# The first row tile of a LayerNorm, FNet and SwiGLU kernel loaded in two halves, with ten warm-up matmuls for eleven

## The chip, the cores and the metric

The kernel runs on one core of a Trainium2 chip. The metric is the device time of one execution in microseconds, given as the median of several runs. The engines in the text are TensorE (PE in the profile, its weight loads PEld), VectorE (DVE), ScalarE (ACT), GpSimd (POOL) and SyncE (SP), which issues most of the loads.

## The reference

`x` has S = 2048 rows of D = 640, F is 1536. `re` and `im` are DFT matrices.

```python
xn = _layernorm(x, axis=-1)                       # (x - m) / sqrt(v + 1e-5) over each row
a = einsum("bsd,ed->bse", xn, dft_hid_re)
b = einsum("bsd,ed->bse", xn, dft_hid_im)
s = einsum("ts,bse->bte", dft_seq_re, a) - einsum("ts,bse->bte", dft_seq_im, b)
h = (_silu(xn @ w_gate) * (xn @ w_up)) @ w_down
return x + s * _silu(h)
```

## The kernel before, in words

The kernel first multiplies the sequence matrices by `xn` (four passes, `seq(0)` to `seq(3)`), then applies the hidden matrices (`hid_s`), then gate, up and down, and adds `x`. Large products are split by Strassen's scheme. Almost every product is made of three matmuls: each operand is split into a high and a low part (tiles `hl`), high by ScalarE (`hl<-raw` or `hl<-xn`, ACTIVATE) and low by VectorE (TENSOR_TENSOR or SCALAR_TENSOR_TENSOR).

A planner (`Plan`) sets the order. Each operation is added with the keys that it reads and writes; `prod` adds one that must be done by a lead time, `step` one of TensorE. In `seq(0)` the plan is `fixed`: operations stand at written times. `pl.alias` lets one key stand for several.

The change lies in `opening()`, which is the start of `seq(0)`. Row tile k of `x` is 128 rows by 640 columns of float32, 320 KB. `OPEN_DMA` lists the first loads in order, all issued by SP: (0,) is row tile 0, (0, 0) the first two blocks of the real sequence matrix `in_cs`, (1, 0) those of the imaginary one, and so on:

```python
OPEN_DMA = ((0,), (0, 0), (1,), (1, 0), (2,), (3,), (0, 1), (1, 1), (4,), (5,), (0, 2), (1, 2), ...)
```

SP's loads use eight semaphores in turn (`DMAHW0` to `DMAHW7`), and a load waits until the one eight places before it, with the same semaphore, has landed.

`layer_norm` works on one row tile: two `bn_stats` of 320 columns each and one `bn_aggr` on VectorE, a square root on ScalarE, one small operation on GpSimd, and small VectorE operations for the scale and the mean. For row tile 0 VectorE then writes `neg`, the negated normalised columns 0 to 255, and normalises the last 128 columns in place. These are the weights of the first six float32 products (kk = 0), which aren't split: three with the block of the real matrix and three with that of the imaginary one. A float32 product is two records in the trace, called passes here. From row tile 1 on (kk = 1 to 7) the operands are split.

Ahead of the first product, `busy(ps[:, 7], n)` issues n warm-up matmuls, 128x512 in bfloat16, of a tile `z` of zeros. Their result isn't used.

All operations are recorded at line 82, so the tiles tell them apart in the profile.

Of the kernel before, what the change touches and what calls it, by code (L numbers as in the profile page):

```python
# [14 lines left out]
P = 128  # L15
# [263 lines left out]
def tile_fnet_swiglu(  # L279
# [16 lines left out]
    nc = Probe(tc.nc)  # L296
# [5 lines left out]
    pl = Plan()  # L302
    mv = one.tile([P, NS, 2], F32, name="mv")
    sm = one.tile([P, 6, NS], F32, name="sm")
    bst = one.tile([P, 2, 2, 6], F32, name="bst")
# [5 lines left out]
    ps = psum.tile([P, 8, TC], F32, name="ps")  # L311
# [3 lines left out]
    def raw(name, a=0, n=None):  # L315
        o, (arena, size) = where[name], pl.size[name]
        n = size - a if n is None else n
        over = arena == "raw" and o >= RAW_KB * 256 - 8
        return space["raw3" if over else arena][:, o + a - over * (RAW_KB * 256 - 8):][:, :n]
# [235 lines left out]
    xn = pl.buf(("xn",), "raw2", NS * D)  # L555
# [5 lines left out]
    def xn_tile(k):  # L561
        return space["xn", k // 8][:, k % 8 * D:k % 8 * D + D]

    def load_x(k, lead, eng):
        pl.prod(lead, lambda: eng.dma_start(xn_tile(k), x[k * P:(k + 1) * P, :]), [], [(xn, k)])

    def layer_norm(k0, n, lead, root, stats, small):

        for k in range(k0, k0 + n):
            for h in range(2):
                pl.prod(stats[k - k0], lambda k=k, h=h: nc.vector.bn_stats(
                    bst[:, k % 2, h], xn_tile(k)[:, h * 320:h * 320 + 320]), [(xn, k)], [("bst", k % 2, h)])
            pl.prod(stats[k - k0], lambda k=k: nc.vector.bn_aggr(
                mv[:, k], bst[:, k % 2].rearrange("p a b -> p (a b)")),
                [("bst", k % 2, 0), ("bst", k % 2, 1)], [("mv", k)])
        y, t, mr, v, nm = (sm[:, i, k0:k0 + n] for i in range(5))
        mean, var = (mv[:, k0:k0 + n, i] for i in range(2))  # L580
        r = rowst[:, 0, NS + k0:NS + k0 + n]
        key = ("sm", k0)
        if small is nc.vector and n == 1:
            sign, half = (-1.0, nm) if k0 == 0 else (1.0, r)
            ops = [
                lambda: nc.scalar.activation(t, var, AF.Sqrt, bias=sm[:, 5, 4:5], scale=0.25),
                lambda: nc.gpsimd.tensor_scalar(v, var, EPS, 0.25 * sign, op0=ALU.add, op1=ALU.mult),
                lambda: small.reciprocal(y, t),
                lambda: small.scalar_tensor_tensor(v, v, y, t, op0=ALU.mult, op1=ALU.subtract if k0 == 0 else ALU.add),
                lambda: small.reciprocal(half, v),  # L590
            ]
            if k0:
                ops.append(lambda: small.scalar_tensor_tensor(mr, mean, -1.0, r, op0=ALU.mult, op1=ALU.mult))
        elif small is nc.vector:
            stt = small.scalar_tensor_tensor
            ops = [
                lambda: nc.scalar.activation(t, var, AF.Sqrt, bias=sm[:, 5, :1]),
                lambda: small.reciprocal(y, t),
                lambda: stt(t, var, EPS, y, op0=ALU.add, op1=ALU.mult),
                lambda: stt(t, t, -0.5, y, op0=ALU.mult, op1=ALU.mult),  # L600
                lambda: stt(r, t, 1.5, y, op0=ALU.add, op1=ALU.mult),
                lambda: stt(mr, mean, -1.0, r, op0=ALU.mult, op1=ALU.mult),
            ]
        else:
            ops = [
                lambda: small.tensor_scalar(v, var, EPS, 1.0, op0=ALU.add, op1=ALU.mult),
                lambda: small.tensor_tensor(y, v, sm[:, 5, 8:8 + n], op=ALU.pow),
                lambda: small.tensor_scalar(nm, mean, -1.0, 0.0, op0=ALU.mult, op1=ALU.add),
                lambda: small.tensor_tensor(t, v, y, op=ALU.mult),
                lambda: small.tensor_tensor(t, t, y, op=ALU.mult),  # L610
                lambda: small.tensor_scalar(t, t, -0.5, 1.5, op0=ALU.mult, op1=ALU.add),
                lambda: small.tensor_tensor(r, y, t, op=ALU.mult),
                lambda: small.tensor_tensor(mr, nm, r, op=ALU.mult),
            ]
        for i, fn in enumerate(ops):
            pl.prod(root[i > 0], fn, [("mv", k) for k in range(k0, k0 + n)], [key])
        if k0 == 0:
            neg = pl.buf(("neg",), "raw", 256)
            minus = lambda to, a, n, scale: small.tensor_scalar(to, xn_tile(0)[:, a:a + n], mean, scale, op0=ALU.subtract, op1=ALU.mult)
            for e in range(2):  # L620
                pl.prod(root[2], lambda e=e: minus(raw(neg, e * P, P), e * P, P, nm), [(xn, 0), key], [(neg, 0)])
            pl.prod(root[2], lambda: small.tensor_scalar(r, nm, -1.0, 0.0, op0=ALU.mult, op1=ALU.add), [key], [key])
            pl.prod(root[2], lambda: minus(xn_tile(0)[:, TC:], TC, P, r), [(xn, 0), key], [(xn, 0, 2)])
            pl.prod(root[2], lambda: small.tensor_tensor(mr, mean, nm, op=ALU.mult), [key], [key])
            pl.prod(lead[0], lambda: nc.scalar.activation(
                xn_tile(0)[:, :TC], xn_tile(0)[:, :TC], AF.Identity, bias=mr, scale=r), [key, (xn, 0), (neg, 0)], [(xn, 0, 0), (xn, 0, 1)])
            return neg
        for k in range(k0, k0 + n):
            pl.prod(lead[k - k0], lambda k=k: nc.scalar.activation(
                xn_tile(k), xn_tile(k), AF.Identity, bias=sm[:, 2, k:k + 1], scale=rowst[:, 0, NS + k:NS + k + 1]),  # L630
                [key, (xn, k)], [(xn, k, c) for c in range(3)])

    def busy(bank, n):

        for _ in range(n):
            nc.tensor.matmul(bank, z[:, :P], z, start=True, stop=True)
# [105 lines left out]
    def seq(k):  # L742
# [112 lines left out]
        def opening():  # L855
# [3 lines left out]
            at = lambda t: -t  # L859
# [7 lines left out]
            def fetch(i, g, t, a=None):  # L867
                src = cs[j, i, g // 2, :, 2 * (g % 2):2 * (g % 2) + 2]
                name = left[i, g]
                if a is None:  # L870
                    pl.prod(at(t), lambda: nc.sync.dma_start(wide(raw(name)), src), [], [(name, 0), (name, 1)])
                else:
                    pl.prod(at(t), lambda: nc.sync.dma_start(raw(name, a * TC, TC), src[:, a]), [], [(name, a)])

            t = -6.0
            for what in OPEN_DMA:
                if len(what) == 1:
                    load_x(what[0], at(t), nc.sync)
                else:
                    fetch(what[0], what[1], t, *what[2:])  # L880
                t += 0.45
            neg = [layer_norm(k0, n, [at(x) for x in apply], [at(x) for x in root], [at(x) for x in stats], nc.vector)
                   for k0, n, stats, root, apply in OPEN_LN][0]
            for kk in range(1, 8):
# [9 lines left out]
            for kk in range(8):  # L894
                for i, banks, db in part if kk < 7 else part[::-1]:
# [6 lines left out]
                    o, a = (s[i, 1], 0) if kk == 1 else (s[i, kk // 2 * 2], kk % 2)  # L902
# [23 lines left out]
        def p2(g):  # L926
            if fresh:
                for kk in (8 + 2 * g, 9 + 2 * g):
                    load_x(kk, 40 + 2 * g, nc.sync)
                layer_norm(8 + 2 * g, 2, *LEAD["xn", 4 + g], nc.gpsimd)  # L930
            return operand("p2", g, load(12, g, 11 if fresh else 20, "raw"))
# [19 lines left out]
        if fresh:  # L951
            opening()
        elif not shared:
            run(("p1", p1, b2, (1, 1)))
# [413 lines left out]
    for i, (t, _, fn, names, _) in enumerate(pl.ops):  # L1368
        if i == turn:
            last.close()  # L1370
            first.close()
            space["hl2"], space["hl3"] = (stack.enter_context(tc.tile_pool(name=name, bufs=1, reuse_waits="tile")).tile(
                [P, TURN_KB * 256], F32R, name=name) for stack, name in ((ctx, "hl2"), (last, "hl3")))
        if i == back:
            last.close()
            space["raw3"] = ctx.enter_context(tc.tile_pool(name="raw3", bufs=1, reuse_waits="tile")).tile(
                [P, TURN_KB * 256], F32, name="raw3")
        if t >= 0 and not started:
            started = True
            busy(ps[:, 7], 11)  # L1380
        fn()


# [38 lines left out]
```

## Time and profile before

| | us |
|---|---|
| median of 3 runs (lowest to highest) | 969.77 (969.72 to 969.93) |
| the profiled execution | 969.83 |
| its span | 967.6 |

| engine | busy us | share of the span |
|---|---|---|
| PE | 961.7 | 99% |
| PEld | 792.0 | 82% |
| DVE | 734.6 | 76% |
| ACT | 488.6 | 50% |
| POOL | 121.3 | 13% |

Times in the profile are microseconds from the start of the span. In the timeline a row is: start, duration, engine (SPq is SyncE's queue), line, operation, output and input tiles, shapes and count, and in brackets the idle time of the engine ahead of it with what ended it. Neighbouring rows of a kind are merged, and how far depends on the stretch that is asked for. In the chain of waits a row is start, duration and what. In a table by stretches of time the row has the length, then the busy time of PE, PEld, DVE, ACT and POOL, the granted clock, the busy share of the DMA engines and what they moved in GB/s.

### The profile page before, as it was taken

The numbers are of one execution on the slowest core, as the hardware profiler recorded it, in microseconds if no ns is written. First come the engines' busy times: TensorE is split into PE (matmuls) and PEld (weight loads), VectorE is DVE, ScalarE is ACT, GpSimd is POOL, SyncE is SP. The second block draws the span as 40 slices with busy tenths as digits, with TensorE's granted clock in tenths as the row PEclk, the third lists the DMA queues.
The fourth block names the chain that finished last, engine by engine and source line by source line (L and its number), as shares of the span: only waits on it lengthen the run. The fifth ranks groups of instructions, "written<-read, shape, count | busy, mean of one in ns | idle before, by whom it ended". The sixth has DMA issues, their size and how long they took to land.

```text
span 967.6 us, 11521 instructions
## 1 busy us (share of the span) xinstructions
PE 961.7 (99%) x4235; PEld 792.0 (82%) x4235; DVE 734.6 (76%) x932; ACT 488.6 (50%) x676; POOL 121.3 (13%) x184
## 2 busy tenths in 40 slices
PE   9999999999999999999999999999999999999998
PEld 5888888888888888888888888888888888888887
DVE  7889668757774687676987898999978666666775
ACT  5686445454545455544356555563446444444341
POOL 1460211011101110111100211210002000000000
PEclk9999999999999999999999999999999999999999
DMA  9997848494938497778673374439699330105793
GB/s 352 283 249 215 233 147 229 152 271 106 231 109 255 109 236 263 208 196 253 170 213 131 141 265 155 168 136 289 222 292 256 99 133 4 55 1 163 240 346 131
DMA packets 64056, 186.50 MB, mean 193 GB/s; under 512 B 6528, under 2 KB 10368, under 8 KB 64000
## 3 DMA queue, kind: packets, MB, share of 16 engines
q1 hardware_dynamic: 45952, 125.45, 39.0%
q0 software_dynamic: 18048, 60.32, 24.2%
q8 instruction: 33, 0.54, 0.2%
q14 instruction: 23, 0.19, 0.1%
HBM read 151.39 MB, written 34.36 MB: 192 GB/s over the span
## 4 chain that ended last, share of the span: by engine, by line
PE 99%; DMA 0%; DVE 0%; ACT 0%; issue 0%; DVEq 0%; ACTq 0%
PE ps L82 99%; DMA xn<-in_x 0%; DVE raw L82 0%; DVE bst L82 0%; DVE sm L82 0%; ACT raw L82 0%; ACT sm L82 0%; DVE mv L82 0%; DVEq L82 0%; ACTq L82 0%
## 5 line engine op out<-in xcount | busy, mean ns | idle before, releaser
L82 PE MATMUL ps<-hl 128*128 128x512 f32 (+1 forms) x3258 | 780.1, 388 | 0.0
L82 PEld LDWEIGHTS ps<-hl 128*128 128x128 f32 x3258 | 610.1, 188 | 126.6 <-DVE hl L82 0.6
L82 DVE TENSOR_TENSOR hl<-raw,hl 128x1024 fp32r<-128x1024 f32 (+5 forms) x360 | 346.5, 994 | 134.3 <-ACT hl L82 94.4
L82 ACT ACTIVATE hl<-raw 128x1024 fp32r<-128x1024 f32 (+6 forms) x416 | 325.0, 826 | 170.3 <-DVE raw L82 84.8
L82 PE MATMUL ps<-hl,hl 128*128 128x512 f32 (+1 forms) x954 | 259.9, 388 | 0.0
L82 ACT ACTIVATE raw<-ps 128x512 f32<-128x512 f32 (+1 forms) x144 | 97.9, 681 | 231.4 <-PE ps L82 225.2
L82 PEld LDWEIGHTS ps<-hl,hl 128*128 128x128 f32 x954 | 179.0, 188 | 36.9
L82 DVE TENSOR_TENSOR raw<-raw 128x1024 f32<-128x1024 f32 (+7 forms) x216 | 178.6, 849 | 19.8 <-ACT raw L82 15.5
L82 DVE TENSOR_TENSOR raw<-ps,raw 128x512 f32<-128x512 f32 (+1 forms) x95 | 77.2, 814 | 48.4 <-PE ps L82 47.6
L82 DVE TENSOR_TENSOR raw<-raw,raw 128x512 f32<-128x512 f32 (+3 forms) x50 | 44.2, 892 | 6.5 <-ACT raw L82 4.3
L82 ACT ACTIVATE hl<-xn 128x1024 fp32r<-128x1024 f32 (+3 forms) x61 | 42.2, 723 | 13.6 <-PE ps L82 9.1
L82 POOL DMA_DIRECT2D p_dram<-raw x24 | 16.4, 686 | 251.4 <-DVE raw L82 215.7
L82 ACT ACTIVATE raw<-raw 128x512 f32<-128x512 f32 (+1 forms) x30 | 21.5, 718 | 46.7 <-DVE raw L82 46.7
L82 DVE TENSOR_TENSOR hl<-xn,hl 128x1024 fp32r<-128x1024 f32 (+3 forms) x50 | 40.8, 833 | 4.0 <-PE ps L82 3.9
L82 POOL DMA_DIRECT2D raw<-in_cs x36 | 32.5, 984 | 57.7 <-DMA raw<-in_cs 29.1
L82 DVE SCALAR_TENSOR_TENSOR hl<-raw,hl 128x256 fp32r<-128x256 f32 (+4 forms) x56 | 32.7, 586 | 4.0 <-ACT hl L82 4.0
L82 POOL DMA_DIRECT2D out<-raw x10 | 6.9, 689 | 226.6 <-DVE raw L82 197.3
L82 POOL DMA_DIRECT2D d_p<-hl x28 | 15.2, 543 | 71.4 <-ACT hl L82 59.6
L82 ACT ACTIVATE xn<-xn,sm,rowst 128x640 f32<-128x640 f32 (+1 forms) x16 | 14.1, 906 | 5.3 <-DVE sm L82 3.6
L82 DVE BATCH_NORM_STATS2 bst<-xn 128x6 f32<-128x320 f32 x32 | 13.7, 479 | 4.0 <-DMA xn<-in_x 4.0
L82 POOL DMA_DIRECT2D y_dram<-raw x12 | 8.2, 683 | 64.6 <-DVE raw L82 46.2
L82 POOL DMA_DIRECT2D raw<-p_dram x8 | 10.1, 1267 | 44.7 <-DVE raw L82 26.3
(42 smaller groups left out, 84.3 us busy)
## 6 DMA issues: line engine op xcount, KB each, us to landing
raw<-in_cs SPq DMA_DIRECT2D x84, 512.0 KB, 7.0
hl<-d_p SPq DMA_DIRECT2D x56, 384.0 KB, 5.0
raw<-in_cs POOLq DMA_DIRECT2D x36, 512.0 KB, 9.8
raw<-in_wb SPq DMA_DIRECT2D x24, 640.0 KB, 4.7
d_p<-hl POOLq DMA_DIRECT2D x28, 384.0 KB, 4.0
p_dram<-raw POOLq DMA_DIRECT2D x16, 512.0 KB, 4.4
raw<-p_dram SPq DMA_DIRECT2D x8, 768.0 KB, 8.5
xn<-in_x SPq DMA_DIRECT2D x16, 320.0 KB, 9.8
```

The costliest lines, as they stand in the source:

```text
L82: return real(*args, **kw)
```

## The change

Row tile 0 is loaded as two halves of 320 columns. Each has a key of its own, (xn, 0, "a") and (xn, 0, "b"); the alias makes an operation that reads the whole tile wait for both, and each of the tile's two `bn_stats` reads one. The other loads follow in the same order. The warm-ups go from eleven to ten.

```diff
+    pl.alias[xn, 0] = [(xn, 0, "a"), (xn, 0, "b")]
+
-    def load_x(k, lead, eng):
-        pl.prod(lead, lambda: eng.dma_start(xn_tile(k), x[k * P:(k + 1) * P, :]), [], [(xn, k)])
+    def load_x(k, lead, eng, h=None):
+        if h is None:
+            pl.prod(lead, lambda: eng.dma_start(xn_tile(k), x[k * P:(k + 1) * P, :]), [], [(xn, k)])
+        else:
+            pl.prod(lead, lambda: eng.dma_start(xn_tile(k)[:, h * 320:h * 320 + 320], x[k * P:(k + 1) * P, h * 320:h * 320 + 320]),
+                    [], [(xn, k, "ab"[h])])
...
                 pl.prod(stats[k - k0], lambda k=k, h=h: nc.vector.bn_stats(
-                    bst[:, k % 2, h], xn_tile(k)[:, h * 320:h * 320 + 320]), [(xn, k)], [("bst", k % 2, h)])
+                    bst[:, k % 2, h], xn_tile(k)[:, h * 320:h * 320 + 320]), [(xn, k) if k else (xn, k, "ab"[h])], [("bst", k % 2, h)])
...
             for what in OPEN_DMA:
-                if len(what) == 1:
+                if len(what) == 1 and what[0] == 0:
+                    for h in range(2):
+                        load_x(0, at(t + 0.2 * h), nc.sync, h)
+                elif len(what) == 1:
                     load_x(what[0], at(t), nc.sync)
...
-            busy(ps[:, 7], 11)
+            busy(ps[:, 7], 10)
```

On SP, at the start of the program, this stood in a row before (`xn_108` is the tile that holds row tiles 0 to 7, 128x1024 a pair of blocks of `in_cs`; what a load waits for stands in brackets):

```order
L82 DMA xn_108<-in_x 128x640
L82 DMA raw<-in_cs 128x1024
L82 DMA xn_108<-in_x 128x640
L82 DMA raw<-in_cs 128x1024
L82 DMA xn_108<-in_x 128x640 x2
L82 DMA raw<-in_cs 128x1024 x2
L82 DMA xn_108<-in_x 128x640 [waits DMAHW0_49]
L82 DMA xn_108<-in_x 128x640 [waits DMAHW1_49]
L82 DMA raw<-in_cs 128x1024 [waits DMAHW2_49]
L82 DMA raw<-in_cs 128x1024 [waits DMAHW3_49]
```

And this stands there now:

```order
L82 DMA xn_108<-in_x 128x320 x2
L82 DMA raw<-in_cs 128x1024
L82 DMA xn_108<-in_x 128x640
L82 DMA raw<-in_cs 128x1024
L82 DMA xn_108<-in_x 128x640 x2
L82 DMA raw<-in_cs 128x1024
L82 DMA raw<-in_cs 128x1024 [waits DMAHW0_49]
L82 DMA xn_108<-in_x 128x640 [waits DMAHW1_49]
L82 DMA xn_108<-in_x 128x640 [waits DMAHW2_49]
L82 DMA raw<-in_cs 128x1024 [waits DMAHW3_49]
L82 DMA raw<-in_cs 128x1024 [waits DMAHW4_49]
```

One load more is issued ahead of all others. The second pair for the imaginary matrix is now the ninth load and waits for the first half of row tile 0; row tile 4 waits for the second half; each load behind waits for the same load as before, under the next semaphore.

On VectorE, at the start of the program, the difference is this:

```order
 L82 BN_STATS bst<-xn_108 128x6 [waits DMAHW0_49]
-L82 BN_STATS bst<-xn_108 128x6
+L82 BN_STATS bst<-xn_108 128x6 [waits DMAHW1_49]
 L82 BN_AGGR mv<-bst 128x2 [waits DVE_49]
 L82 RECIPROCAL sm<-sm 128x1 [waits Activation_49]
```

The second statistic has a wait of its own, for the second half; the order of VectorE's instructions is the same, as it is on ScalarE and GpSimd. On TensorE one weight load and one matmul of `z` are gone from the front.

## The prediction, made before the changed kernel was run

> **What bounds the kernel now.** I read the head of the page first, then the chain of waits in order of time, then the list of waits of TensorE's weight loads, and last the timeline of the first 20 us and the DMA table, because the change lies there.
>
> ```profile
> span 967.6 us, 11521 instructions
> ```
> ```profile
> 0.73 3.01 DMA xn<-in_x
> ...
> 3.76 0.90 DVE bst L82 x2
> ...
> 6.06 0.36 DVE raw L82
> ...
> 6.46 956.86 PE ps L82 x4224
> ...
> 964.22 0.42 DVE raw L82
> ```
> ```profile
> PEld ps L82 <- DVE raw L82: 1.2, 1, 1.2
> PEld ps L82 <- DMA raw<-in_cs: 0.8, 1, 0.8
> PEld ps L82 <- DVE hl L82: 0.6, 2, 0.4
> ```
>
> The chain (start, duration, what) has 6.46 us of opening, 957 us of matmuls in one piece and 0.9 us of end. The opening is row tile 0: its load, its statistics, and the normalised columns `neg` that the first matmul takes as weights. The second view (us in total, times, longest) shows that behind the first matmul TensorE's weight loads waited for a load of `in_cs` once and for VectorE twice. The timeline puts these waits in the first 17 us:
>
> ```profile
> 8.71 0.59 PE L82 MATMUL ps<-raw,xn 128*128 128x512 f32 x1
> ...
> 9.25 0.30 PEld L82 LDWEIGHTS ps<-raw 128*128 128x128 f32 x2 [0.78 <-DMA raw<-in_cs]
> 9.79 0.19 PEld L82 LDWEIGHTS ps<-raw 128*128 128x128 f32 x1 [0.24 <-issue]
> 10.22 0.19 PEld L82 LDWEIGHTS ps<-raw 128*128 128x128 f32 x1 [0.24 <-issue]
> ...
> 11.53 10.63 PE L82 MATMUL ps<-hl 128*128 128x512 f32 x43
> ...
> 15.61 0.41 PEld L82 LDWEIGHTS ps<-hl 128*128 128x128 f32 x2
> 16.42 0.19 PEld L82 LDWEIGHTS ps<-hl 128*128 128x128 f32 x1 [0.40 <-DVE hl L82]
> ```
>
> Row tile 0 needs two products of six float32 passes each, one every 0.43 us (9.79 to 10.22): first with the block of `in_cs` for the real part, then with that for the imaginary part. The last pass of the first product starts at 8.71, so the next could start at 9.14, but its weight load starts at 9.25 and its first pass 0.11 us behind that: TensorE loses 0.22 us to a load of `in_cs` that has only just landed. The second loss is at 16.42: two loads from 15.61, at 10.63 / 43 = 0.25 us or a little less apiece, would put the next near 16.07, so 0.35 us go to a split on VectorE. Behind 16.42 no wait of TensorE is left. So the time is fixed by the moment at which matmuls run from 16.42 on, and a gain ahead of it counts only as far as it gets past these two waits.
>
> What sets them is the stream of loads:
>
> ```profile
> DMA  0028999899989999999999999999999999999999
> GB/s 0 0 41 180 409 353 344 302 303 242 274 215 289 347 392 424 419 419 408 421 406 438 423 420 419 391 410 432 411 416 424 420 419 426 413 426 426 413 426 409
> ...
> raw<-in_cs SPq DMA_DIRECT2D x12, 512.0 KB, 8.7
> ```
> ```profile
> 10.25 0.89 DVE L82 BATCH_NORM_STATS2 bst<-xn 128x6 f32<-128x320 f32 x2 [0.20 <-DMA xn<-in_x]
> ...
> 12.25 1.06 ACT L82 ACTIVATE hl<-raw 128x1024 fp32r<-128x1024 f32 x1 [0.49 <-DMA raw<-in_cs]
> ...
> 13.22 0.91 ACT L82 ACTIVATE xn<-xn,sm,rowst 128x640 f32<-128x640 f32 x1
> ...
> 14.61 0.42 DVE L82 SCALAR_TENSOR_TENSOR hl<-xn,hl 128x256 fp32r<-128x256 f32 x1 [0.28 <-ACT hl L82]
> ...
> 15.15 1.22 DVE L82 TENSOR_TENSOR hl<-raw,hl 128x1024 fp32r<-128x1024 f32 x1
> ```
>
> The first two lines cut 0 to 25 us in 40 slices of 0.625 us: from the fifth slice (2.5 us) on, the DMA engines are nine tenths busy, and a load lands some 8.7 us behind its issue, though issuing takes under half a us. The split that TensorE waits for at 16.42 ends at 15.15 + 1.22 = 16.37. Its queue goes back over VectorE 14.61 (which waited for ScalarE), ScalarE 13.22 and 12.25 to a landing of `in_cs` near 12.2, and over VectorE 10.25 to the landing of row tile 2. None of these two begins with row tile 0.
>
> **The change part by part.** *The first half.* The issue rows:
>
> ```profile
> 0.73 0.38 SPq L82 DMA_DIRECT2D xn<-in_x  x1
> 1.16 0.42 SPq L82 DMA_DIRECT2D raw<-in_cs  x1
> 1.63 0.42 SPq L82 DMA_DIRECT2D xn<-in_x  x1
> 2.10 0.43 SPq L82 DMA_DIRECT2D raw<-in_cs  x1
> ```
> ```profile
> 2.50:3.00 0.50, 0.50 (x3) 0.16 (x2) 0.00 (x0) 0.00 (x0) 0.00 (x0) 1.00 1.05 404
> 3.00:3.50 0.50, 0.50 (x3) 0.23 (x2) 0.00 (x0) 0.00 (x0) 0.00 (x0) 1.00 1.04 377
> ```
>
> The tile has 128 rows of 2,560 B, 328 KB, and lands at 0.73 + 3.01 = 3.74. Half of it is 164 KB, at the 404 and 377 GB/s of the stretches in which it arrives (last column) 0.42 us. So the first half lands near 3.32. Its bounds are 3.27 (half a us is the most that this count gives) and 3.74 (the engines finish both halves together).
>
> *The second half and everything behind it.* No row has the price of one more load of the same bytes. From below it is 0: no bytes are added, and the halves are in the queue before the engines get to them. From above it is the step of SP's issue rows, 0.43 to 0.47 us (0.73, 1.16, 1.63, 2.10), if each load behind starts as much later as it is issued. I take 0.1, near the lower end: cs for the second product is issued at 2.10 and lands near 9.2, a queue of 7 us, in which a later issue is not felt. The second half then lands at 3.84, the `in_cs` blocks and the row tiles 0.1 later each. On SP the later loads wait for the landing of the load eight places before them; that pairing stays, only the last of the first eight gets a new wait, for the first half, over by 3.3 while SP reaches it past 4.
>
> *Statistics.* Two at 0.45 us (0.90 for both): the first from 3.34 to 3.79, the second from 3.86 to 4.31, against 4.66 before. Gain 0.35 us, with 0.45 as the upper bound (second half in time) and 0 as the lower (it lands at 4.2). The small operations up to 6.46 keep their 1.8 us, and the first matmul comes at 6.11. The block of `in_cs` that it also needs is there:
>
> ```profile
> 1.31 4.87 PE L82 MATMUL ps<-z 128*128 128x512 bf16 x11 [1.31 <-POOL sm L82]
> ...
> 4.69 0.15 PEld L82 LDWEIGHTS <-z 128*128 128x128 bf16 x1 [0.28 <-issue]
> 5.12 0.15 PEld L82 LDWEIGHTS <-z 128*128 128x128 bf16 x1 [0.28 <-issue]
> ...
> 5.26 0.63 ACT L82 ACTIVATE hl<-raw 128x512 fp32r<-128x512 f32 x1
> ...
> 7.09 0.88 DVE L82 BATCH_NORM_STATS2 bst<-xn 128x6 f32<-128x320 f32 x2
> ```
>
> ScalarE reads that block at 5.26, and even 0.47 later is 5.73.
>
> *One warm-up fewer.* Each takes 0.43 us (4.69 to 5.12). Eleven end at 1.31 + 4.87 = 6.18, ten at 5.75, so neither holds up a matmul at 6.11 by more than 0.07. What the tenth-for-eleventh costs otherwise is the clock, a rival below; here it costs nothing.
>
> *Where the 0.35 us go.* The first product's six passes end at 9.14 - 0.35 = 8.79. The second still needs the block that landed near 9.2, now 9.3: TensorE waits 0.67 instead of 0.22, and the second product starts 0.1 later than before. VectorE takes the statistics of row tile 1 (7.09) a little earlier, at best when that tile lands, but what they lead to is not what TensorE waits for. At 16.42 the split is due 0.1 later, TensorE arrives 0.1 later, and the wait keeps its 0.35.
>
> **Sum:** 0.35 gained ahead of the first matmul, 0.35 given back at 9.25, 0.1 lost to the stream: +0.1 us. The profiled execution took 969.83 us (span 967.6 and 2.2 around it), the median of the runs is 969.77. That gives 969.87; I write 969.85.
>
> **The rivals.**
>
> *The gain passes.* The block for the second product and those that lead to 16.42 would have to land a third of a us earlier. For it speaks that the engines move only 215 to 303 GB/s between 4.4 and 8.1 us against 420 later, so a changed order of packets could make up time; against it, that no byte is removed and no load is issued earlier. Price: -0.35, 969.4. All three waits gone would be 0.35 + 0.22 + 0.35 = 0.92, 968.9, which is the floor and still within 0.2%.
>
> *The loads come late.* Each load behind starts 0.43 to 0.47 later, as it is issued: both waits end so much later, +0.45, 970.2. The queue of 7 us speaks against it, the busy figure of 8 (not 9) in some slices for it.
>
> *The clock (the other side).* The warm-ups pay 0.43 us for 512 columns, the split products from 11.53 on 0.25. So TensorE starts at about half its rate and gets faster somewhere behind 5.12, though the granted clock reads 1.00 throughout. Before, 4.87 us of matmuls and a break of 0.28 us led up to 6.46, and the passes behind ran at 0.43. Now there are 4.44 us, a break of about 0.36, and the passes. If what is missing is made up by the first pass, that costs under 0.43, and the wait at 9.3 hides it. If the break starts the count again and 4.87 us are needed once more, about six passes run at 0.86. A slow pass costs 0.43; 0.67 of it is hidden at 9.3 and 0.35 at 16.42: 6 x 0.43 - 1.02 + 0.1 = +1.66, 971.4. From seven slow passes on (+2.1) the kernel is slower by over 0.2%; all twelve would be +4.2, 974.0. Against it: the break grows by only 0.1 us, and the three runs before lie within 0.21 us, so that nothing in the opening seems to hang on chance.
>
> The Trainium skill, "TensorE: Matmul & The Clock Gate", Part 1, speaks against this edit: the array runs at half clock until it has been busy through a window of about 3.4 us, and that window is free-running, so a burst that leaves part of it idle may have to wait for the next one. By that page's figure, one missed window would be four slow passes, 4 x 0.43 - 1.02 + 0.1 = +0.8, or 970.6, as an estimate. The trace agrees in that the eleven warm-ups from 1.31 to 6.18 are all slow and the passes from 6.46 are not; where the window lies it does not show.
>
> **How the numbers follow.** The wait swallows the gain (969.6 to 970.1): 0.68. The gain passes: 0.14. The loads come late: 0.10. The clock, with one or more slow passes not hidden: 0.06, about half of it near or beyond seven passes. Something not thought of: 0.02. The first holds 969.6 to 970.1; to leave out no more than two in ten the range takes in the middle of the second and all of the third: 969.3 to 970.4. What a measurement here can tell from no change is taken as 0.2%, 1.94 us, so only the clock and the unforeseen reach past it: faster 0.01, same 0.95, slower 0.04.
>
> **What would show it.** In the profile after: two single statistics on VectorE, the first near 3.3 and the second near 3.9; the first float32 weight load near 6.1; the wait for `in_cs` at 9.3 grown from 0.78 to about 1.2 us; the wait for VectorE at 16.4 to 16.5 still there, and from it on the same matmuls. I am wrong in a step if the second half lands past 4.2 (no gain to lose), if the weight load behind the first product comes before 9.1 (the block was not set by the stream), or if passes stand 0.86 us apart (the clock).

## The result, and the profile after

The changed kernel takes 971.46 us (median of 16 runs, 971.04 to 972.69), the kernel before 969.82 (16 runs, 969.52 to 970.09). The ratio is 1.0019, with a 95% interval of 1.0012 to 1.0025: 1.64 us slower. That is inside the 0.2% that was taken as the same, and outside the forecast range, which ended at 970.4. The profiled execution took 971.47 us with a span of 969.3. In one round of the experiments below three executions, one of an experiment and two of the kernel before, took 1634 to 1984 us and are left out of the times.

The chain of waits of the changed kernel (start, duration, what) no longer begins with row tile 0:

```profile
span 969.3 us, 11520 instructions
...
2.58 7.62 DMA raw<-in_cs
...
10.25 953.86 PE ps L82 x4218
...
965.01 0.43 DVE raw L82
```

A block of `in_cs`, issued at 2.58, now leads to the matmuls. The timeline of the opening, in the rows that answer to those of before:

```profile
3.06 0.93 DVE L82 BATCH_NORM_STATS2 bst<-xn 128x6 f32<-128x320 f32 x2 [3.06 <-DMA xn<-in_x]
...
6.68 0.63 ACT L82 ACTIVATE hl<-raw 128x512 fp32r<-128x512 f32 x1 [2.06 <-DMA raw<-in_cs]
6.76 0.30 PEld L82 LDWEIGHTS ps<-raw 128*128 128x128 f32 x2 [1.92 <-DVE sm L82]
6.79 1.96 PE L82 MATMUL ps<-raw 128*128 128x512 f32 x4 [1.04 <-DMA raw<-in_cs]
...
7.57 0.89 DVE L82 BATCH_NORM_STATS2 bst<-xn 128x6 f32<-128x320 f32 x2 [1.06 <-DMA xn<-in_x]
...
10.25 0.30 PEld L82 LDWEIGHTS ps<-raw 128*128 128x128 f32 x2 [1.47 <-DMA raw<-in_cs]
10.78 0.19 PEld L82 LDWEIGHTS ps<-raw 128*128 128x128 f32 x1 [0.24 <-issue]
11.21 0.19 PEld L82 LDWEIGHTS ps<-raw 128*128 128x128 f32 x1 [0.24 <-issue]
...
11.01 0.89 DVE L82 BATCH_NORM_STATS2 bst<-xn 128x6 f32<-128x320 f32 x2 [0.47 <-DMA xn<-in_x]
...
13.05 1.06 ACT L82 ACTIVATE hl<-raw 128x1024 fp32r<-128x1024 f32 x1 [0.58 <-DMA raw<-in_cs]
...
17.22 0.19 PEld L82 LDWEIGHTS ps<-hl 128*128 128x128 f32 x1 [0.23 <-DVE hl L82]
```

The statistics run in one piece from 3.06 to 3.99, 0.67 us earlier than before. But every load behind row tile 0 lands late. By the trace's semaphore events (16 for a load, of which the last counts) the first block of `in_cs` lands at 6.66 (5.24 before; ScalarE takes it at 6.68 and the first matmul at 6.79, which names the load as what it waited for), row tile 1 at 7.54 (6.86), the block of the second product at 10.21 (9.21), row tile 2 at 10.99 (10.23), the second block at 13.03 (12.23). The weight load that follows the last wait comes at 17.22 for 16.42: 0.80 us.

That is half of what was lost. The other half is behind the last matmul. The rows are the last matmul of each kernel, SP's wait for the last stores (us in total, times, longest) and the end of SP's final waits (a DRAIN at 966.7 and at 968.3), of before and then of the changed kernel:

```profile
963.03 0.28 PE L82 MATMUL ps<-hl,hl 128*128 128x256 f32 x1
...
SPq L1418 <- DMA out<-raw: 0.7, 1, 0.7
...
L1418 SPq DRAIN  x3: 7/7/7, 966.7 to 967.0; - x3
```
```profile
963.82 0.28 PE L82 MATMUL ps<-hl,hl 128*128 128x256 f32 x1
...
SPq L1427 <- DMA out<-raw: 1.5, 1, 1.5
...
L1427 SPq DRAIN  x3: 7/7/7, 968.3 to 968.6; - x3
```

The last matmul is 0.79 us later, the end of the final waits 1.6. In the trace SP ends the program with one check per semaphore, in a fixed order with those of its loads and stores from the first to the eighth. The starts of the last checks in the trace, in us, with the place of the semaphore where it matters:

```
before:  ... 965.44 (5th)  965.51 (6th)  965.87 (7th)  966.61 (8th, that of the last store) | drain 966.67
after:   965.88  967.44 (1st, that of the last store)  967.50  967.57  967.65  967.73  968.09  968.17  968.23 | drain 968.31
```

Before, the last store had the eighth semaphore. The checks of the seven others ran while it was on its way, and it landed at 966.59. With one load more every later load and store moves on by one semaphore, so the last store has the first one. It lands at 967.42, 3.60 us behind the start of the last matmul (3.56 before), but SP has stood at its check since 965.88, and seven checks come behind: 967.44 to 968.23, 0.80 us.

So 0.8 + 0.8 = 1.6 us is the theory for this execution: the loads behind an issue more come late, and the row of final checks comes late. The rivals were the warm-up that was taken out (the clock), and the halves themselves.

### The profile page after: what moved, and what is told of

Read it like the earlier page. It is cut to its first block, busy times and chain, and to the rows that moved or that the text cites. A ratio compares the mean times of both kernels' runs of the same rounds, so it can differ in the third digit from the quotient of the medians.

```text
span 969.3 us, 11520 instructions
## 1 busy us (share of the span) xinstructions
PE 961.1 (99%) x4234; PEld 791.6 (82%) x4234; DVE 735.0 (76%) x932; ACT 488.5 (50%) x676; POOL 121.5 (13%) x184
## 4 chain that ended last, share of the span: by engine, by line
PE 98%; DMA 1%; SPq 0%; DVE 0%; ACT 0%; issue 0%
PE ps L82 98%; DMA raw<-in_cs 1%; SPq L82 0%; DVE raw L82 0%; ACT raw L82 0%
## 5 line engine op out<-in xcount | busy, mean ns | idle before, releaser
L82 POOL DMA_DIRECT2D raw<-in_xt x6 | 6.9, 1296 | 72.1 <-DVE raw L82 72.1
```

Source lines behind the costliest of these rows:

```text
L82: return real(*args, **kw)
```

## The experiments

All ratios are against the kernel before, run in turn on the same chip. It took 969.70 us beside the ten warm-ups, the one late load, the semaphore put back and the small load second; 969.84 beside the small load ninth and the three with ScalarE's queue; 969.83 beside the four late loads and the later issue; 969.71 beside the last two. Effects of a few tenths of a us are near the width of the intervals, so the traces stand beside them.

**Ten warm-ups alone.**

```diff
-            busy(ps[:, 7], 11)
+            busy(ps[:, 7], 10)
```

> The kernel before with ten warm-up matmuls for eleven and nothing else. If the changed kernel is slower because its loads come late and its end waits longer (my theory now: about +0.8 us in the opening and +0.8 us at the end), this takes as long as the kernel before, within 0.2 us, and its float32 passes stand 0.43 us apart. If the clock is the cause (the rival of the prediction), this has up to +1.66 us and passes 0.86 us apart.

969.82 us, ratio 1.0003 (0.9994 to 1.0012). The last weight load of the program starts within 0.12 us of before and passes stand 0.43 us apart. The warm-up is not what cost 1.6 us. But three of eleven executions took 970.5 to 971.3, which none of before did; this is followed up below.

**One small load late in the program.** It sits where the plan's time passes 850 us; the experiments with a count n of late loads use the same lines.

```diff
+        if t >= 850 and late:
+            for _ in range(late):
+                late -= 1
+                nc.sync.dma_start(sm[:, late // 2, late % 2 * 8:late % 2 * 8 + 8], x_in[:P, late * 8:late * 8 + 8])
         fn()
```

> The kernel before with one load more on SP (128 rows of 32 B into a tile that is no longer used), some 850 us into the program, where the DMA engines are nearly idle. It moves every later load and store to the next of the eight semaphores, so that the last store has the first semaphore, which SP checks early in its row of final waits, and seven checks come behind it. If this row is what the changed kernel loses at its end: +0.8 us (the trace of the changed kernel has 0.80 from the check of the last store to the last check, the one before 0.07), the opening as before. If the end only follows the opening: 0.

970.50 us, ratio 1.0009 (1.0000 to 1.0018); all eleven executions (970.24 to 970.72) lie above all 33 of before (969.41 to 970.22). The opening is as before. SP's wait for the last store reads as in the changed kernel:

```profile
SPq L1422 <- DMA out<-raw: 1.5, 1, 1.5
```

So +0.8 us comes from the place of the last store in the row of checks, without any change in the opening.

**Four small loads late.** The same lines with `late = 4`: the last store has the fourth semaphore.

> The kernel before with four small late loads on SP, so that the last store has the fourth semaphore and four checks come behind its own for none before and seven in the changed kernel. If the checks behind it are what is paid: between 0.25 (four at 0.065) and 0.55 us (with one of the slow ones of 0.36 among them), against 0.8 with seven. If any shift costs the same: 0.8.

970.12 us, +0.29, ratio 1.0003 (0.9994 to 1.0012).

```profile
SPq L1422 <- DMA out<-raw: 0.9, 1, 0.9
```

The trace has four checks behind that of the last store, from 966.68 to 966.93, about 0.06 us each: 0.25 us. A slow check of some 0.36 us, which the rows of before and of the changed kernel have too, ran here while the store was on its way. What is paid is the checks that are left when the last store lands.

**The changed kernel with the last store's semaphore put back.** The same lines with `late = 7` in the changed kernel.

> The changed kernel with seven such small loads on SP at the same late place, so that the last store has the eighth semaphore again, as before the change. If the row of final waits costs 0.8 us: 0.8 us faster than the changed kernel, so +0.8 us against before, all of it in the opening (the weight load behind the last split near 17.2 us for 16.4). If the end only follows the opening: as the changed kernel, +1.6 us.

970.63 us, ratio 1.0012 (1.0003 to 1.0020): +0.93 against before, where the changed kernel had +1.64, so 0.71 us are back.

```profile
16.98 0.53 PEld L82 LDWEIGHTS ps<-hl 128*128 128x128 f32 x3 [0.52 <-DVE hl L82]
```

The weight load behind the last wait of the opening starts at 16.98: the end is repaired, the opening is not. How much the opening loses differs from execution to execution. It was 0.80 us in the trace of the changed kernel and is 0.56 in this one, whose execution took 970.33; five of the eleven took 970.95 to 972.23, and none of these has a trace.

**One small load second, the halves left out.**

```diff
                     load_x(what[0], at(t), nc.sync)
+                    if what[0] == 0:
+                        pl.prod(at(t + 0.2), lambda: nc.sync.dma_start(pad, x_in[:P, :8]), [], [("pad", 0)])
```

> The kernel before, row tile 0 whole, with one small load (128 rows of 32 B) as the second load of SP, and the seven late ones, so that the last store keeps its semaphore. It has the one issue more of the changed kernel, not its halves. If one issue more ahead of the other loads is what makes them late (each issued 0.47 us later): the blocks of in_cs land 0.5 to 1.4 us later, +0.5 to +0.9 us in all. If it is the halves themselves (packets of 1,280 B, done early, which leave engines without work): the blocks land within 0.2 us of before and the time is within 0.2 us.

970.39 us, +0.69, ratio 1.0009 (1.0000 to 1.0018). Row tile 0 is whole, and yet the loads behind it land like those of the changed kernel:

```profile
6.54 0.63 ACT L82 ACTIVATE hl<-raw 128x512 fp32r<-128x512 f32 x1 [1.31 <-DMA raw<-in_cs]
...
9.84 0.30 PEld L82 LDWEIGHTS ps<-raw 128*128 128x128 f32 x2 [1.19 <-DMA raw<-in_cs]
...
12.78 1.06 ACT L82 ACTIVATE hl<-raw 128x1024 fp32r<-128x1024 f32 x1 [0.44 <-DMA raw<-in_cs]
16.95 0.30 PEld L82 LDWEIGHTS ps<-hl 128*128 128x128 f32 x2 [0.36 <-DVE hl L82]
```

4 KB more in the queue, but one issue more ahead of the blocks, is enough for most of the loss in the opening. The halves aren't needed for it.

**The same small load ninth.**

```diff
+                    if what[0] == 4:
+                        pl.prod(at(t - 0.2), lambda: nc.sync.dma_start(pad, x_in[:P, :8]), [], [("pad", 0)])
                     load_x(what[0], at(t), nc.sync)
```

> The kernel before with the one small load as the ninth load of SP for the second, just ahead of row tile 4, and the seven late ones. SP waits for landings from there on, and no wait of TensorE hangs on what comes behind. If only the loads issued ahead of the ones that TensorE needs count: within 0.2 us of before. If any load more in the opening costs: +0.5 to +0.7 as in the second place.

969.64 us, ratio 0.9998 (0.9989 to 1.0006). Behind the eighth load SP only waits for landings, and one more costs nothing. So it is the place ahead of the loads that TensorE needs that counts, not their number.

**A later issue without a load more.** GpSimd writes into the place of the first block, and the block's load has to wait for it.

```diff
     nc.gpsimd.memset(sm[:, 5, 8:], -0.5)
+    nc.gpsimd.memset(raw(("c", 1), 0, 96), 0.0)
```

> The kernel before, with the same loads, but the second load of SP (the block of in_cs for the first product) waits for a small GpSimd write to its place, so that it and all loads behind are issued about 0.4 us later with no load more and nothing changed at the end. If the later issue is what makes the blocks late: +0.4 to +0.7, as with the small load in the second place. If it is one load more in the engines' queues: within 0.2 us of before.

970.29 us, +0.46, ratio 1.0004 (0.9995 to 1.0014), where the lower end of the interval is no change. The issues came 0.34 us later for the block and 0.25 for those behind it. In the trace the block of the second product lands near 9.8, and the last wait of the opening ends at 17.09:

```profile
1.50 0.33 SPq L82 DMA_DIRECT2D raw<-in_cs  x1
1.89 0.42 SPq L82 DMA_DIRECT2D xn<-in_x  x1
2.35 0.43 SPq L82 DMA_DIRECT2D raw<-in_cs  x1
...
9.84 0.30 PEld L82 LDWEIGHTS ps<-raw 128*128 128x128 f32 x2 [1.41 <-DMA raw<-in_cs]
...
17.09 0.19 PEld L82 LDWEIGHTS ps<-hl 128*128 128x128 f32 x1 [0.51 <-DVE hl L82]
```

The first block lands near 5.4, as before, so not every landing follows the issue. In the median a quarter to a third of a us of later issue costs a little more than itself, but three executions of this kernel lie at 969.5 to 969.8 and the others at 970.2 and above, so it doesn't happen each time. Taken alone this run doesn't prove the later issue; the next one does more.

**The second half from ScalarE's queue.** SP then issues every other load when it did before. The square root that loads ScalarE's table is moved behind it, and seven late loads put the end back.

```diff
-                        load_x(0, at(t + 0.2 * h), nc.sync, h)
+                        load_x(0, at(t + 0.2 * h), (nc.sync, nc.scalar)[h], h)
```

> The changed kernel with the second half of row tile 0 issued by ScalarE's queue at the start (ScalarE's square-root table is loaded behind it), so that SP issues every other load when it did before the change; seven small late loads give the last store the eighth semaphore again. If one issue more on SP ahead of the blocks of in_cs is the whole cost in the opening: 969.7 +- 0.2, the blocks land near 5.3 and 9.2, and the first float32 pass comes near 5.8. If it is the halves: +0.8 as in the run with the halves and the semaphores put back.

970.10 us, ratio 1.0002 (0.9993 to 1.0011).

```profile
6.26 0.30 PEld L82 LDWEIGHTS ps<-raw 128*128 128x128 f32 x2 [1.41 <-DVE raw L82]
...
9.34 0.30 PEld L82 LDWEIGHTS ps<-raw 128*128 128x128 f32 x2 [1.06 <-DMA raw<-in_cs]
```

The opening's loss is gone: the second product's weight load starts at 9.34, and the last weight load of the program is 0.08 us earlier than before. The halves and the one load more are still there, and only SP's later issue is not. So neither the halves nor the number of loads makes the blocks late. Nor do they bring anything: both halves land near 3.6, the first pass comes at 6.26 for the 5.8 expected, and the time isn't below that of before. The +0.26 of the median isn't explained: in the profiled execution the last store took 2.2 us from issue to landing for 1.9 before. Whether that has to do with the change stays open. Where the engines' time differs shows in the stretches from 3.0 to 4.0 us (last two columns: busy share of the DMA engines and GB/s), first of the changed kernel, then of this one:

```profile
3.00:3.50 0.50, 0.50 (x3) 0.23 (x2) 0.44 (x2) 0.00 (x0) 0.00 (x0) 1.00 0.58 225
3.50:4.00 0.50, 0.50 (x3) 0.22 (x2) 0.48 (x2) 0.00 (x0) 0.00 (x0) 1.00 0.75 246
```
```profile
3.00:3.50 0.50, 0.50 (x3) 0.23 (x2) 0.00 (x0) 0.00 (x0) 0.00 (x0) 1.00 1.12 383
3.50:4.00 0.50, 0.50 (x3) 0.22 (x2) 0.43 (x2) 0.00 (x0) 0.00 (x0) 1.00 1.00 352
```

In the changed kernel the DMA engines stand partly idle there (0.58 and 0.75; before, 1.04 in the first of these stretches). By the trace only about eight packets are in flight from 3.2 to 3.8, for about 16 in the kernel before: row tile 0 is done early, and the next block, issued at 1.64 for 1.16, keeps no more than that many going yet. In the kernels with the small load second and with the wait such gaps come later, behind 4.5 and 5.0 us (busy share 0.52 and 0.63). The queue of 7 us that the prediction relied on is not an unbroken one.

**The first two pairs of blocks from ScalarE's queue**, row tile 0 whole, then the same with the halves.

```diff
-                    pl.prod(at(t), lambda: nc.sync.dma_start(wide(raw(name)), src), [], [(name, 0), (name, 1)])
+                    pl.prod(at(t), lambda: (nc.scalar if g == 0 else nc.sync).dma_start(wide(raw(name)), src), [], [(name, 0), (name, 1)])
```

> The kernel before with the first pair of blocks of each matrix issued by ScalarE's queue at the start, beside SP's row tiles, so that the first eight loads are all issued some 0.9 us earlier; the number of loads and the last store's semaphore stay. If the issue sets when the blocks land: they land 0.3 to 0.9 us earlier and the time falls by 0.3 to 0.5 us. If only the bytes in the engines do: within 0.2 us.

> The changed kernel with the same two loads on ScalarE's queue and the last store's semaphore put back. It has what the change was to have, an earlier first statistic, without the later issue of the blocks. If the issue was the cost: as fast as the run with these loads on ScalarE's queue and row tile 0 whole, or up to 0.3 us faster than it. If the halves cost something themselves: 0.3 to 0.8 us slower than it.

ScalarE's square root stands behind these loads, and the second of the two has the seven late loads. 972.65 us, ratio 1.0026 (1.0017 to 1.0034), and 974.39 in five executions, ratio 1.0047 (1.0034 to 1.0059). Both expectations were wrong, and their grounds with them: an earlier issue from a second queue doesn't help here. Timeline and stretches of the first of the two:

```profile
5.16 0.49 DVE L82 BATCH_NORM_STATS2 bst<-xn 128x6 f32<-128x320 f32 x1 [5.16 <-DMA xn<-in_x]
...
7.86 0.30 PEld L82 LDWEIGHTS ps<-raw 128*128 128x128 f32 x2 [2.58 <-DVE raw L82]
...
9.82 0.34 PEld L82 LDWEIGHTS ps<-raw,xn 128*128 128x128 f32 x1 [0.52 <-DVE mv L82]
10.68 0.34 PEld L82 LDWEIGHTS ps<-raw,xn 128*128 128x128 f32 x1 [0.52 <-issue]
```
```profile
8.00:9.00 1.00, 1.00 (x3) 0.38 (x4) 0.96 (x6) 0.39 (x1) 0.00 (x0) 0.83 1.02 390
9.00:10.00 1.00, 1.00 (x3) 0.48 (x2) 0.60 (x3) 0.72 (x2) 0.19 (x1) 0.50 1.03 420
10.00:11.00 1.00, 1.00 (x3) 0.48 (x2) 0.83 (x5) 0.11 (x1) 0.00 (x0) 0.50 1.05 429
11.00:12.00 1.00, 1.00 (x2) 0.35 (x2) 1.00 (x3) 0.97 (x2) 0.00 (x0) 0.50 0.99 399
12.00:13.00 1.00, 1.00 (x3) 0.38 (x2) 0.95 (x4) 1.00 (x4) 0.26 (x1) 0.96 1.03 412
```

Row tile 0 lands at 5.1 for 3.7, beside the block issued at the same 0.73, which lands at 5.3; the first pass comes at 7.86. The Trainium skill, "DMA: Bandwidth & Descriptors", section "Issuing engines are not separate DMA queues", says that transfers of all issuers run on the same 16 engines and interleave, and that a second issuer saves only issue time. The trace agrees in that the two loads land together, and here the price, 1.4 us on the load that is waited for, was above the 0.4 to 0.9 us by which the two blocks were issued earlier. And here the clock is seen: passes stand 0.86 us apart (9.82 to 10.68), and the granted clock reads half from 9 to 12 us, which the trace's clock records put at 8.66 to 12.08. With the halves on top, the second half landed near 7.0, so that the passes began at 9.4, and these were slow as well.

**Eight warm-ups, and eleven with the halves.** Two more runs on the clock.

> The kernel before with eight warm-ups for eleven, which leaves TensorE idle for about 1.5 us ahead of the first float32 pass where it was 0.3. With ten warm-ups eight of eleven executions took as long as before and three took 970.5 to 971.3, while none of some 80 executions of the kernel before took over 970.3. If the clock is let go later in some executions for want of warm-up: most or all executions in the upper group, with float32 passes 0.86 us apart in them, median +0.7 to +1.7. If the three were chance: within 0.2 us of before.

> The changed kernel with eleven warm-ups again. The loads and the last store's semaphore stay as changed, so that by those two causes the median is that of the changed kernel, 971.4 +- 0.2. If the lost warm-up has a share in the changed kernel's slower executions (three of 16 took 972.1 to 972.7, two of them at a lower mean clock): none of these over 972, and a median lower by up to 0.2.

With eight warm-ups for eleven and nothing else: 969.95 us, ratio 1.0005 (0.9996 to 1.0014). Seven of eleven executions took 969.35 to 969.96, as before; four took 970.7 to 972.4. The profiled one was among these, at 970.68, with passes 0.85 us apart up to 8.90 and 0.43 from 9.62 on:

```profile
7.20 0.34 PEld L82 LDWEIGHTS ps<-raw 128*128 128x128 f32 x1 [0.52 <-DVE sm L82]
8.05 0.34 PEld L82 LDWEIGHTS ps<-raw 128*128 128x128 f32 x1 [0.52 <-issue]
8.90 0.34 PEld L82 LDWEIGHTS ps<-raw,xn 128*128 128x128 f32 x1 [0.52 <-DVE sm L82]
9.62 0.19 PEld L82 LDWEIGHTS ps<-raw,xn 128*128 128x128 f32 x1 [0.38 <-issue]
10.05 0.19 PEld L82 LDWEIGHTS ps<-raw 128*128 128x128 f32 x1 [0.24 <-issue]
```

The changed kernel with eleven warm-ups took 971.41 us, ratio 1.0019 (1.0010 to 1.0028), as with ten, and still had two executions of eleven over 972. So the warm-up has no share in the 1.64 us. With eight warm-ups the trace shows passes at half rate, and the median of the kernel is hardly moved. That the three executions over 970.4 with ten warm-ups had the same cause is likely, but none of them has a trace.

No version beat the kernel before.

## Why the prediction was wrong, point by point

- *What bounds the kernel.* Right: behind the last wait of the opening the matmuls run on as before (16.42 and 17.22 to the last at 963.03 and 963.82), so what is lost in the opening is lost once and in full.
- *The halves and the statistics.* Forecast were a first half at 3.32, a second at 3.84 and a gain of 0.35 us. Measured were 3.03, 3.47 and 0.67. The gain was larger than forecast, and it was lost ahead of the first matmul, not behind it: the first product needs its block of `in_cs`, at 6.68, which the prediction had put at 5.73 at the latest.
- *The step that failed in the opening* is the term for everything behind the second half. It was taken as 0.1 us, near the lower end of 0 to 0.47. The blocks and row tiles came 0.7 to 1.4 us later, above the upper end, and the last wait 0.80. The ground for 0.1, that a queue of 7 us hides a later issue, was wrong: one issue of 4 KB in the second place gave +0.69, the later issue alone +0.46, and with SP's issues as before the blocks were in time. The upper bound assumed that a load lands later by as much as it is issued later, 0.43 to 0.47. Of the 16 landings of the block for the second product the first came 0.35 us later than before (7.15 to 7.50), and the last, which is waited for, 1.00 (9.21 to 10.21). Why the parts of a load drift apart stays open; the idle stretch from 3.2 to 3.8 is a candidate, but the trace's packets don't say which engine took them. The rival "the loads come late" named the mechanism, at 0.45 for 0.8 us.
- *The step that was missing* is the end. The prediction saw that each later load moves to the next semaphore, said that the pairing stays, and looked no further. It stays for the loads. For the row of final checks it doesn't, and that was 0.8 us, shown by a load late in the program (+0.80), four (+0.29), and seven in the changed kernel (0.71 back).
- *One warm-up fewer costs nothing.* Right in the median (969.82 with ten; and 971.41 for the changed kernel with eleven, 971.46 with ten). The clock as a rival had priced this change at 971.4, next to the result, but its sign, passes 0.86 us apart, is missing: 10.78 to 11.21 is 0.43. And the trace's clock records give the full clock from 6.27 before and from 5.67 in the changed kernel, in both ahead of the first pass (6.46 and 6.79). A time that fits is no proof of its cause. The mechanism itself does exist here, as the slow passes with eight warm-ups and with the blocks on a second queue show. The Trainium skill, "TensorE: Matmul & The Clock Gate", Part 1, has the clock go by windows of about 3.4 us. The stretches with the blocks on a second queue agree on the length: (1 - 0.83) x 2 + 3 + (1 - 0.96) x 2 = 3.4 us at half clock.
- *The wait for the block at 10.25* grew to 1.47 us, for 1.2 forecast, by a later block and not by an earlier first product.

## What to carry to other kernels

One load more has two prices besides its bytes: the issue that all loads behind it on that queue wait for, and a shift of everything that is dealt out in turn, down to the checks at the program's end. Ask of each load ahead of a wait when the last part of it lands, not only when it is issued, and put an extra one behind the loads that are waited for, where it was free here. When an edit changes a count, follow that count to the last instruction.

## What the runs showed of the hardware that was not expected

- A check of a semaphore at the end takes SP 0.06 to 0.09 us, and one in the rows of before and of the changed kernel some 0.36. In the order in which they stand, those behind the last landing are paid in full: 0.25 us for four, 0.80 for seven, by the traces.
- The granted clock reads 1.00 ahead of the trace's first clock record, whatever the rate. With eight warm-ups the first record stands at 9.48, and it is there that the passes turn from slow to fast (8.90, 9.62, 10.05); in the column all of it reads 1.00. So the distance of the matmuls tells of the clock in the opening, where that column doesn't.
- The first record can be late with eleven warm-ups too: with four late loads it stands at 7.15, and the first pass took 0.94 us (6.30 to 7.24, for 6.46 to 6.99 before). The wait for the block of the second product hid it.
